# A searched instruction sequence found again under later ends, with ordered start-up work and repeated weight rows loaded as two transfers

## The chip, the cores and the metric

The kernel runs on one core of a Trainium2 chip. A core has five engines that run their own instruction streams: TensorE (PE, matrix products, with a separate row PEld for weight loads), VectorE (DVE), ScalarE (ACT), GpSimd (POOL) and SyncE (SP), which here only issues transfers. Transfers run on 16 DMA engines that all queues of the core share. The metric is device time in microseconds of one execution; the profile is one execution recorded by the hardware.

## What is computed

Two pre-normalised blocks over 2048 rows of 448 features, in bfloat16:

```python
h  = x + A(layernorm(x))        # A: 16 heads of 28; query s looks at keys s, s-2, ..., s-14
h2 = h + B(layernorm(h))
# A:  q,k,v = x@wqkv ; softmax over 8 dilated keys ; o @ wo
# B:  h  = gelu(layernorm(x) @ w1)
#     g0..g3 = the four 112-column quarters of h, shifted by -1, +1, -2, +2 rows
#     x1 = x + concat(g0..g3) @ w2
#     return x1 + gelu(layernorm(x1) @ w3) @ w4        # 448 -> 1792 -> 448
```

## The kernel before

The kernel is written as about 1,090 operations ("ops") that a recording layer collects. Each op has an engine, one or more instructions and the set of ops it depends on. The list `ORDER` near the top of the file is one fixed permutation of all ops, found by an offline search; `schedule` (line 251) walks it, puts each op at the end of its engine's queue, hands out buffers, and estimates start and end times with constants such as `dma_bw` and `lag`. These estimates decide which of the free buffers an op gets and where dummy matmuls ("fillers", `S.filler`) go into gaps of TensorE; the queues themselves follow `ORDER`. `_emit_plan` then derives the semaphore waits. So on each engine the order is frozen, an instruction that waits holds everything behind it on that engine, and nothing is decided at run time. All instructions are recorded through one line, L1039, which is why the profile's groups are told apart by their buffers.

The 2048 rows are 16 tiles of 128, handled in four groups `t` of four tiles. The string `PLAN` names the stages. For attention: `N1 t` (statistics and normalising of x into the buffer `lntm`), `A1 t` (turn `lntm` into `actT`, then queries and keys into `arena`), `V t` (values into `vt`, then copied by transfers into the windowed form `vw`), `A2 t` (on DVE products `qk_r` of 4096 columns, summed per head on PE with the 0/1 matrix `zc`; then softmax and `pb`), `A3 t` (block-diagonal weights `bd_r`, times `vw`) and `O t` (times `wo_s`, plus the residual, into `xin`). For the second block: `B1 t` with `M t` (first MLP with `w1_s`), and then, in units `u` of 3, 4, 4, 4 and 1 tiles, `B2 u`/`T u` (times `w2_s` and the second normalising), `W3 u` (448 to 1792, into `h3T`) and `B3 u` (1792 to 448, into `ost`, then out). In both kernels `phase_W3` forms its products only for units of more than one tile (line 968), so for the last single tile the 448-to-1792 product is left out and `B3` reads what its `h3T` buffers hold.

"Turning" (features onto partitions) is done either on PE (`t` in `TURN`) or by a transposing transfer from SP (`d`): A1 of groups 2 and 3, all of B1, and three of the five B2 units use the transfer. Two strings choose an engine per tile or group: `NORM` for the normalising (`a` ACT, `v` DVE) and `STATS` for the statistics.

The contraction length 448 is three chunks of 128 rows and a rest of 64. `contract` (line 689) runs two products' rests side by side on the two 64-row halves of PE, so the last 64 rows of a weight have to lie on partitions 0 to 63 and again on 64 to 127. `dma_rows` (line 540) loads a weight that way: one transfer `main` for the three chunks, one transfer `rest` for the repeated rows. `rest` reads the same 64 rows twice through an access pattern whose outermost step is `[0, 2]`. The loads are `wqk`, `wv` (from SP), and `w1`, `w3` (from GpSimd), with the rests `wqkr`, `wvr`, `w1r`, `w3r`. For the combined rest of queries and keys, `setup` has GpSimd copy two column blocks of the repeated rows of `wqkv_s` into `wr_s`; a PE group of seven half-height products (64 rows) in A1 waits for these copies.

GpSimd also builds `bmask` (eight dependent `affine_select`s), `zc` (through `indj`, which lives in the buffer `ls`), the mask row of the first window (`maskrow`, ones and -30000s, read by one small matmul of A2 0), and paddings; then it issues the weight loads, the `vw` copies and later the adds of the second residual. In `ORDER` of the kernel before, these set-up instructions are interleaved with the transfers, and `mhalf` and part of `bmask` come as late as after the first `vw` copies.

Of the kernel before, what the change touches and what calls it, by code (L numbers as in the profile page):

```python
# [14 lines left out]
NORM = {'N0': 'aava', 'N1': 'avvv', 'B1': 'avva', 'B2': 'vaava'}  # L15
STATS = {'N1': 'vvva', 'B1': 'vvav', 'B2': 'aavaa'}
# [43 lines left out]
RUNS = {'A3': '1111', 'W3': '24324'}  # L60
# [124 lines left out]
class _Sched:  # L185
# [13 lines left out]
    def group(self, eng, insts, dur, lag=60.0, chan=None, nbytes=0, table=None, after=(), hold=None, pe=()):  # L199
        op = _Op(len(self.ops), self.prio, eng, insts, float(dur), float(lag))  # L200
# [48 lines left out]
    BEHIND = 400.0  # L249

    def schedule(self, dma_bw=190.0, dma_fixed=2000.0, table_load=1300.0):
# [8 lines left out]
        n = len(self.ops)  # L260
# [11 lines left out]
        for idx in ORDER:  # L272
# [13 lines left out]
            if op.is_dma:  # L286
# [3 lines left out]
                if op.nbytes:  # L290
                    dma_free = max(st + op.dur, dma_free) + op.nbytes / dma_bw
                    op.t1 = dma_free + dma_fixed + op.lag
                    if op.eng == "sp":
                        dma_land = max(dma_land, op.t1)
                else:
                    op.t1 = st + op.dur + op.lag
# [102 lines left out]
def bass_sequential_preLN__sliding_local_dilated__mixer_s_mlp__prompt_kernel(  # L399
# [33 lines left out]
    with ExitStack() as es:  # L433
# [106 lines left out]
        def dma_rows(chan, dst, src, lo, n, eng="sp", behind=(), parts=False):  # L540

            last = src[384:448, lo:lo + n]
            def main():
                dma(chan, dst[:, 0:3, :], src[0:384, lo:lo + n].rearrange("(c k) n -> k c n", k=128), 384 * n * 2, eng=eng, behind=behind)
            def rest():
                dma(chan + "r", dst[:, 3, :], bass.AP(last.tensor, last.offset, [[0, 2]] + [list(d) for d in last.ap]),
                    128 * n * 2, eng=eng, behind=behind)
            if parts:
                return main, rest
            main()  # L550
            rest()
# [166 lines left out]
        def setup(after):  # L718
# [3 lines left out]
            for lo in (0, 1):  # L722
                later("tensor_copy", 350, out=wr_s[:, :, 64 * lo:64 * lo + 64], in_=wqkv_s[:, :, 384 + D * lo:448 + D * lo])
# [357 lines left out]
```

## Time and profile before

| what | value |
|---|---|
| median of 3 runs | 209.94 us (207.58, 209.94, 212.35) |
| the profiled execution | 207.0 us; its span from first to last instruction 205.3 us |
| mean granted TensorE clock | 0.983 |
| PE busy | 189.5 us, 1599 matmuls |
| ACT, DVE, POOL busy | 140.2, 123.5, 50.5 us |
| moved by DMA | 17.33 MB in 27079 packets |

In the views that follow, a row of the timeline is: start in us from the first instruction, duration in us, engine, line, operation, output<-inputs, shape, number of merged instructions, and in brackets the idle time of the engine just before it and what ended that. A row of a group is: engine, operation, buffers, shapes, count | busy us in all, mean ns of one | idle us before them. A row of "stretches" is: the window, its length, then the busy time of each engine with the number of its instructions, the granted TensorE clock, the mean busy share of the 16 DMA engines, and GB/s. A row of DMA issues is: output<-input, queue, count, KB of each, median us from issue to landing.

### The profile page before, as it was taken

How to read it: one execution, taken by the hardware profiler on the slowest of the kernel's cores; microseconds unless marked ns; L12 is line 12 of the kernel's file. 1: busy time of each engine (PE TensorE's matmuls, PEld its weight loads, DVE VectorE, ACT ScalarE, POOL GpSimd, SP SyncE). 2: the span in 40 equal slices, each digit the busy share in tenths (PEclk: the TensorE clock that was granted, in tenths of full speed). 3: DMA queues.
4: the chain of work that ended last, by engine and by line, in shares of the span. 5: the costliest groups of instructions: out<-in, count | busy, mean ns of one | idle time of the engine just before them, and what ended most of it. 6: DMA issues, size and time to landing. Idle time of an engine off the chain costs nothing.

```text
span 205.3 us, 3977 instructions
## 1 busy us (share of the span) xinstructions
PE 189.5 (92%) x1599; PEld 90.0 (44%) x1599; DVE 123.5 (60%) x225; ACT 140.2 (68%) x313; POOL 50.5 (25%) x94
## 2 busy tenths in 40 slices
PE   6869699975999499899999999999999999999996
PEld 2445233432434145454455544435544444444563
DVE  7759677998299869999487877570034314310024
ACT  4918699796379669999986975289942497155221
POOL 1239948000630000030083070110050005500040
PEclk9999999997599999999999999999999999999999
DMA  5945359398399500001329060000561002401003
GB/s 156 289 136 154 96 114 221 102 73 84 90 282 362 90 3 0 3 8 27 76 69 151 9 127 24 3 0 0 102 147 48 0 0 51 97 26 45 0 0 112
DMA packets 27079, 17.33 MB, mean 84 GB/s; under 512 B 20443, under 2 KB 25499, under 8 KB 27061
## 3 DMA queue, kind: packets, MB, share of 16 engines
q1 hardware_dynamic: 24388, 9.77, 24.8%
q0 software_dynamic: 2672, 7.32, 12.8%
q8 instruction: 12, 0.20, 0.4%
q14 instruction: 7, 0.05, 0.1%
HBM read 7.91 MB, written 1.84 MB: 47 GB/s over the span
## 4 chain that ended last, share of the span: by engine, by line
PE 69%; ACT 14%; DMA 7%; DVE 5%; issue 4%; POOL 1%; DVEq 0%; POOLq 0%; ACTq 0%
PE ps L1039 69%; DMA actT<-lntm 6%; ACT arena L1039 5%; ACT actT L1039 3%; ACT lntm L1039 2%; DVE qk_r L1039 2%; ACT vt L1039 1%; DMA xin<-in_A_x_dram 1%; DVE lntm L1039 1%; POOL arena L1039 1%; ACT xin L1039 1%; ACT rs_x L1039 1%; DVE st L1039 1%; DVE mx L1039 0%; DVE ls L1039 0%
## 5 line engine op out<-in xcount | busy, mean ns | idle before, releaser
L1039 PE MATMUL ps<-actT,arena 128*128 128x512 bf16 (+4 forms) x348 | 69.0, 364 | 1.6 <-POOL arena L1039 1.6
L1039 PE MATMUL ps<-arena,h3T 128*128 128x448 bf16 (+1 forms) x238 | 46.5, 342 | 0.0
L1039 ACT ACTIVATE h3T<-ps 128x512 bf16<-128x512 f32 (+1 forms) x56 | 28.5, 577 | 24.8 <-PE ps L1039 24.6
L1039 PEld LDWEIGHTS ps<-actT,arena 128*128 128x128 bf16 (+1 forms) x348 | 27.8, 97 | 37.4 <-issue 7.7
L1039 ACT ACTIVATE arena<-ps 128x512 bf16<-128x512 f32 (+4 forms) x64 | 31.3, 524 | 11.6 <-PE ps L1039 10.8
L1039 POOL TENSOR_TENSOR arena<-arena,xin 128x448 f32<-128x448 f32 x16 | 16.4, 1044 | 87.3 <-DVE lntm L1039 49.5
L1039 DVE TENSOR_TENSOR qk_r<-arena 128x4096 bf16<-128x4096 bf16 (+1 forms) x16 | 32.0, 2018 | 1.4 <-PE ps L1039 1.2
L1039 PEld LDWEIGHTS ps<-arena,h3T 128*128 128x128 bf16 x238 | 22.8, 98 | 20.5 <-issue 0.8
L1039 DVE SCALAR_TENSOR_TENSOR ost<-ps,mrs,arena 128x448 bf16<-128x448 f32 (+1 forms) x17 | 11.0, 653 | 29.3 <-POOL mrs L1039 14.0
L1039 ACT ACTIVATE actT<-ps 128x512 bf16<-128x512 f32 (+2 forms) x25 | 15.7, 644 | 14.6 <-PE ps L1039 14.3
L1039 DVE TENSOR_TENSOR bd_r<-arena,bmask 80x2048 bf16<-80x2048 bf16 x16 | 19.6, 1267 | 2.1 <-ACT arena L1039 2.0
L1039 DVE BATCH_NORM_STATS2 st<-xin 128x6 f32<-128x448 bf16 x24 | 14.5, 618 | 6.7 <-ACT xin L1039 4.5
L1039 PE MATMUL ps<-wo_s,actT 128*128 128x448 bf16 x64 | 16.7, 388 | 1.6 <-ACT actT L1039 1.4
L1039 DVE SCALAR_TENSOR_TENSOR arena<-xin,rs_y,ps 128x448 f32<-128x448 bf16 x16 | 10.5, 677 | 12.0 <-PE ps L1039 11.9
L1039 PE MATMUL ps<-actT,w_s 128*112 128x512 bf16 (+1 forms) x64 | 14.7, 388 | 3.1 <-DMA actT<-lntm 3.1
L1039 PE MATMUL ps<-w_s,arena 112*128 112x448 bf16 x64 | 13.8, 353 | 0.3 <-ACT arena L1039 0.3
L1039 POOL DMA_DIRECT2D vw<-vt x15 | 9.0, 603 | 20.7 <-PE ps L1039 18.1
L1039 PE MATMUL ps<-arena,actT 128*128 128x448 bf16 (+1 forms) x64 | 12.6, 354 | 0.5 <-ACT arena L1039 0.5
L1039 POOL TENSOR_TENSOR rs_y<-rs_x,mhalf 128x4 f32<-128x4 f32 (+1 forms) x5 | 4.7, 935 | 28.2 <-DVE rs_x L1039 24.4
L1039 DVE COPY lntm<-lntm 128x256 bf16<-128x256 bf16 (+2 forms) x16 | 4.0, 249 | 11.0 <-ACT lntm L1039 10.7
L1039 PEld LDWEIGHTS ps<-actT,w_s 128*112 128x112 bf16 (+1 forms) x64 | 6.6, 129 | 9.1 <-DMA actT<-lntm 3.5
L1039 ACT ACTIVATE lntm<-arena,nm 128x448 bf16<-128x448 f32 x12 | 7.9, 667 | 3.7 <-DVE nm L1039 3.7
(74 smaller groups left out, 200.1 us busy)
## 6 DMA issues: line engine op xcount, KB each, us to landing
out_dram<-ost SPq DMA_DIRECT2D x15, 112.0 KB, 1.7
arena<-in_B_w_dram POOLq DMA_DIRECT2D x1, 1568.0 KB, 9.3
arena<-in_B_w_dram POOLq DMA_DIRECT2D x1, 1344.0 KB, 11.3
vw<-vt POOLq DMA_DIRECT2D x4, 320.0 KB, 4.5
vw<-vt POOLq DMA_DIRECT2D x4, 256.0 KB, 4.7
xin<-in_A_x_dram SPq DMA_DIRECT2D x2, 448.0 KB, 10.2
xin<-in_A_x_dram SPq DMA_DIRECT2D x3, 224.0 KB, 3.0
arena<-in_A_wqkv_dram SPq DMA_DIRECT2D x1, 672.0 KB, 6.1
```

Of the source, the lines that this page charges most:

```text
L1039: inst = getattr(eng, meth)(**kw)
```

## The change

The search has been run again after the estimates in `schedule` were altered, so `ORDER` is a new permutation, and with it some strings. What else is edited:

```diff
-NORM = {'N0': 'aava', 'N1': 'avvv', 'B1': 'avva', 'B2': 'vaava'}
-STATS = {'N1': 'vvva', 'B1': 'vvav', 'B2': 'aavaa'}
+NORM = {'N0': 'vavv', 'N1': 'avvv', 'B1': 'avva', 'B2': 'vaavv'}
+STATS = {'N1': 'vvva', 'B1': 'vvav', 'B2': 'aaaaa'}
...
-RUNS = {'A3': '1111', 'W3': '24324'}
+RUNS = {'A3': '1111', 'W3': '23334'}
...
-        op = _Op(len(self.ops), self.prio, eng, insts, float(dur), float(lag))
+        op = _Op(len(self.ops), self.prio, eng, insts, float(dur), float(lag + self.LATE * (eng == "pool" and chan is None)))
...
+    SHARED = 1500.0
+    LATE = 300.0
+
+    def schedule(self, dma_bw=240.0, dma_fixed=2000.0, table_load=1300.0):
...
-                    op.t1 = st + op.dur + op.lag
+                    op.t1 = st + op.dur + op.lag + (self.SHARED if dma_free > st else 0.0)
...
             def rest():
-                dma(chan + "r", dst[:, 3, :], bass.AP(last.tensor, last.offset, [[0, 2]] + [list(d) for d in last.ap]),
-                    128 * n * 2, eng=eng, behind=behind)
+                for h in (0, 64):
+                    dma(chan + "r%d" % h, dst[h:h + 64, 3, :], last, 64 * n * 2, eng=eng, behind=behind)
...
-            for lo in (0, 1):
-                later("tensor_copy", 350, out=wr_s[:, :, 64 * lo:64 * lo + 64], in_=wqkv_s[:, :, 384 + D * lo:448 + D * lo])
+            n_ = len(S.ops)
...
                 later("tensor_copy", 168, out=zc[:, :, e, 16 * e:16 * e + 16], in_=indj)
+            for lo in (0, 1):
+                later("tensor_copy", 350, out=wr_s[:, :, 64 * lo:64 * lo + 64], in_=wqkv_s[:, :, 384 + D * lo:448 + D * lo])
...
-
+            early = [op for op in S.ops if op.eng == "pool" and (op.idx < S.phase0 or op.idx >= n_)]
+            for d, op in zip(early, early[1:]):
+                op.odeps.add(d)
+            rest.append(early[-1])
+
+        rest = []
...
-            dma("vwa%d" % sl, vw[PADK:KW, sl, 0:8:2, :], vt[0:64, sl, :, :], 64 * 4096, 600.0, "pool")
+            dma("vwa%d" % sl, vw[PADK:KW, sl, 0:8:2, :], vt[0:64, sl, :, :], 64 * 4096, 600.0, "pool", behind=rest[t:])
...
+        early = [op for op in S.ops if op.eng == "sp"]
+        for d, op in zip(early, early[1:]):
+            op.odeps.add(d)
```

In words: the planner now lets GpSimd's computing end 0.3 us later and a transposing transfer 1.5 us later when ordinary transfers are still under way, and takes 240 instead of 190 GB/s for loads. The repeated rows come by two plain transfers of 64 partitions each. SP's thirteen start-up loads are issued in the order in which they are written, which is the first three x transfers, then `wqk`, then the other x tiles and rests, with the last eight x tiles at the end. GpSimd's set-up runs in the order written: `ident`, `epsilon`, `mhalf`, paddings, all of `bmask`, then (after the normalising of the fourth tile, as before) `indj` and `zc`, the two `wr_s` copies, the mask row, paddings, and only then the loads of `wo`, `w1`, `w2`; the first `vw` copies come behind those.

In the new sequence, as it is built: `w3`'s main load stands on GpSimd right behind the first three `vw` copies, ahead of the copy `vwa0` (before, it was the last load, behind `w4`); the mask-row matmul stands behind V 1 instead of ahead of it; three products of A1 3 stand between the first two groups of A3 0, and so need the second transposing transfer earlier; the five filler matmuls of the kernel before are gone; W3 of unit 1 runs its 14 products in three rounds instead of four, W3 of unit 3 in three instead of two.

More of the change, by code (lines that the diff above doesn't have):

```diff
@@ L249 @@
     BEHIND = 400.0
-    def schedule(self, dma_bw=190.0, dma_fixed=2000.0, table_load=1300.0):
+    SHARED = 1500.0
+    LATE = 300.0
+    def schedule(self, dma_bw=240.0, dma_fixed=2000.0, table_load=1300.0):
         children = [[] for _ in self.ops]
@@ L818, in phase_V @@
                 dma("vwp%d" % sl, vw[0:PADK, sl, 0, :], vt[112:128, 1 - sl, 3, :], PADK * 1024, 600.0, "pool")
-            dma("vwa%d" % sl, vw[PADK:KW, sl, 0:8:2, :], vt[0:64, sl, :, :], 64 * 4096, 600.0, "pool")
-            dma("vwb%d" % sl, vw[0:KW, sl, 1:8:2, :], vt[48:128, sl, :, :], 80 * 4096, 600.0, "pool")
-            last = dma("vwc%d" % sl, vw[0:PADK, sl, 2:8:2, :], vt[112:128, sl, 0:3, :], 16 * 3072, 600.0, "pool")
+            dma("vwa%d" % sl, vw[PADK:KW, sl, 0:8:2, :], vt[0:64, sl, :, :], 64 * 4096, 600.0, "pool", behind=rest[t:])
+            dma("vwb%d" % sl, vw[0:KW, sl, 1:8:2, :], vt[48:128, sl, :, :], 80 * 4096, 600.0, "pool", behind=rest[t:])
+            last = dma("vwc%d" % sl, vw[0:PADK, sl, 2:8:2, :], vt[112:128, sl, 0:3, :], 16 * 3072, 600.0, "pool", behind=rest[t:])
             for which, load in zip(LOADS, (load_w3, load_w4)):
```

76 rows, old and new, of the table ORDER are left out of this document.

## The prediction

> **What bounds the kernel now.** I read the slices of the page first, then the chain of waits in order of time, then stretches of 10 us.
>
> ```profile
> PEclk9999999997599999999999999999999999999999
> PE 69%; ACT 14%; DMA 7%; DVE 5%; issue 4%; POOL 1%; DVEq 0%; POOLq 0%; ACTq 0%
> ...
> 89.73 113.03 PE ps L1039 x751
> ...
> 40.00:50.00 10.00, 6.27 (x128) 3.05 (x126) 9.98 (x8) 8.69 (x21) 0.00 (x0) 0.93 1.11 87
> 50.00:60.00 10.00, 9.88 (x89) 4.00 (x91) 5.21 (x12) 5.12 (x14) 4.76 (x7) 0.73 0.51 139
> 60.00:70.00 10.00, 7.28 (x56) 3.04 (x52) 9.93 (x10) 9.87 (x21) 0.00 (x0) 1.00 1.09 285
> 90.00:100.00 10.00, 10.00 (x76) 4.89 (x75) 9.08 (x10) 9.64 (x28) 0.00 (x0) 1.00 0.28 55
> ```
>
> There are two halves. From 89.73 on, the chain is PE alone for 113.03 us: no wait is left there, and a new order of the same matmuls cannot shorten it. Before that the chain changes hands, and PE loses time in four places: at the start, near 21 us, at 47 to 57 us (the only dip of the granted clock) and at 67 us. What the change is worth is decided there, and a gain there reaches the end whole, because behind it PE runs without a gap.
>
> **The start (A).**
>
> ```profile
> 9.79 2.78 PE L1039 MATMUL ps<-actT,arena 128*128 128x256 bf16 x24
> ...
> 13.33 0.73 POOL L1039 COPY arena<-arena 128x256 bf16<-128x256 bf16 x2 [3.12 <-DMA arena<-in_A_wqkv_dram]
> ...
> 14.12 3.08 PE L1039 MATMUL ps<-actT,arena 64*128 64x512 bf16 x16 [1.55 <-POOL arena L1039]
> ...
> 12.00:14.00 2.00, 0.57 (x6) 0.26 (x3) 1.09 (x4) 0.00 (x0) 0.67 (x2) 1.00 0.24 58
> 42.00:44.00 2.00, 2.00 (x37) 0.74 (x36) 1.98 (x3) 1.88 (x6) 0.00 (x0) 1.00 0.12 50
> ...
> arena<-in_B_w_dram POOLq DMA_DIRECT2D x1, 1344.0 KB, 11.3
> ...
> arena<-in_B_w_dram POOLq DMA_DIRECT2D x1, 448.0 KB, 12.8
> ```
>
> PE has its 24 full products done at 12.57 and stands 1.55 for the half-height ones; GpSimd's two copies stand 3.12 before that, for the repeated rows of `wqk`. While those are awaited the DMA engines are 0.24 busy; while the rest of `w3` is under way (42 to 44), 0.12, which of 16 is two engines. And that rest of `w3` took 12.8 us to land, longer than the 1344 KB of the same weight. So a repeated load, with its outermost step of 2, seems to run on two engines. As two transfers of 64 partitions it should use many. By the 1344 KB row, 448 KB would take some 4 us; I hold 4 to 12.8 as bounds, take the lower, and so let the rows of `wqk` land with the rest of it, about 4 us earlier.
>
> [...]
>
> What is late next is GpSimd itself, since the copies now stand behind `bmask`, `indj` and `zc`:
>
> ```profile
> 8.94 0.51 POOL L1039 MEMSET arena<- 1x512 bf16 x1 [7.27 <-ACT lntm L1039]
> ...
> 14.55 0.19 POOL L1039 TENSOR_SCALAR_AFFINE_SELECT ls<-ls 128x16 bf16<-128x16 bf16 x1
> ...
> L1039 POOL TENSOR_SCALAR_AFFINE_SELECT ls<-ls 128x16 bf16<-128x16 bf16 (+1 forms) x5 | 3.9, 798 | 0.0
> L1039 POOL TENSOR_SCALAR_AFFINE_SELECT bmask<-bmask 80x64 bf16<-80x64 bf16 x8 | 3.5, 432 | 0.5
> ```
>
> GpSimd idled 7.27 until the fourth tile was normalised (8.94); into that the eight `bmask` steps (3.5) fit. Behind it come five `indj` steps: 3.9 as measured, but their mean of 0.80 holds some that ran beside DVE's large products, and 0.19 is what one took alone; so 1.0 to 3.9, plus the fills and copies of `zc`, below 1. Start no later than 8.9, copies 0.73 long: they end between 11.6 and 14.4. DVE has no large product then, so I take the lower end, and the 1.55 goes. The fourth tile's and the first tile's normalising also move from ACT to DVE, which is quicker at it:
>
> ```profile
> L1039 ACT ACTIVATE lntm<-xin,nmr,rs_y 128x448 bf16<-128x448 bf16 x11 | 8.1, 753 | 0.1
> L1039 DVE TENSOR_SCALAR lntm<-xin,mv,rs_y 128x448 bf16<-128x448 bf16 x13 | 4.4, 393 | 3.4 <-ACT rs_y L1039 3.4
> ```
>
> 0.36 less for each of two, 0.7. **A is 2.3** (bounds 0, and 3.0 with twice the 0.7, since three products now also run ahead of the fourth tile's turn).
>
> **The mask row (B).**
>
> ```profile
> 22.67 0.09 POOL L1039 MEMSET arena<- 1x2 bf16 x1
> ...
> 22.91 0.37 PE L1039 MATMUL ps<-arena 1*32 1x512 bf16 x1 [1.94 <-ACT vt L1039]
> ...
> 25.04 0.54 ACT L1039 ACTIVATE vt<-ps 128x448 bf16<-128x448 f32 x1 [1.75 <-PE ps L1039]
> ```
>
> PE stands 1.94 before the mask matmul. The row blames an ACT eviction, but the matmul reads the mask row, whose last memset ended at 22.76; V 1 stands behind it, and ACT then waits 1.75 for V 1. In the new order the mask row is set right behind the copies and its matmul comes after V 1. Late next is ACT, whose evictions the first bracket names. Bounds 0 and 1.94; **I take 1.5**.
>
> **The stall at 47 (C).**
>
> ```profile
> q8 instruction: 1, 0.02, 36.2%
> ...
> 34.31 0.90 POOL L1039 DMA_DIRECT2D arena<-in_B_w_dram  x1
> ...
> 46.39 0.93 PE L1039 MATMUL ps<-wo_s,actT 128*128 128x448 bf16 x4 [0.92 <-ACT actT L1039]
> ...
> 47.44 0.33 PE L1039 MATMUL ps<-bd_r,vw 80*32 80x64 bf16 x20
> 50.12 0.35 PE L1039 MATMUL ps<-bd_r,vw 80*32 80x64 bf16 x12 [2.35 <-issue]
> ...
> 50.40 1.68 PE L1039 MATMUL ps<-wo_s,actT 128*128 128x448 bf16 x4
> 50.52 0.60 ACT L1039 ACTIVATE actT<-ps 128x512 bf16<-128x512 f32 x1 [1.54 <-PE ps L1039]
> ```
>
> PE stops inside a group of 32 whose operands are all there: 20 run, then 2.35 pass with no releaser. The first line is the DMA queue of instructions in the stretch from 47.5 to 47.7: one packet, just as PE runs dry. I read it as a late instruction fetch, held up behind the rest of `w3` (issued at 34.31, landed 12.8 later at 47.1) and the transposing transfer that met it. The clock then falls: the same four products take 1.68 instead of 0.93, and at 0.73 the stretch from 50 to 60 loses 2.7 us of full-speed time. With the split the cause is gone. Not all comes back, because ACT sets the pace there: it lost 1.54 of the 2.35, and half of the 2.7. **C is 1.54 + 1.35 = 2.9** (bounds 0 and 5.05).
>
> [...]
>
> **The wait for B1's turn (D).**
>
> ```profile
> 63.85 6.45 DMA actT<-lntm
> ...
> actT<-lntm SPq DMA_TRANSPOSE x9, 4.6
> ```
>
> This transfer ran beside the loads of `w3` and `w4` (285 GB/s in that stretch) and took 6.45; the median of nine is 4.6. `w3` now comes with the first `vw` copies, and `w4` earlier by as much as A3 0 does. **I take 1.0** of the difference (bounds 0 and 1.85).
>
> **What is added.** The `w3` load moves on GpSimd's queue ahead of `vwa0`, which A3 0 needs:
>
> ```profile
> 28.94 0.70 POOL L1039 DMA_DIRECT2D vw<-vt  x1 [2.59 <-ACT vt L1039]
> ...
> 43.90 0.43 PE L1039 MATMUL ps<-bd_r,vw 80*32 80x64 bf16 x32
> ...
> 53.32 1.82 POOL L1039 DMA_DIRECT2D vw<-vt  x3 [18.11 <-PE ps L1039]
> ...
> vw<-vt POOLq DMA_DIRECT2D x4, 256.0 KB, 4.7
> ...
> DMA to landing us min/median/max: 6.0/6.4/10.6
> ```
>
> The `vw` copies began at 28.94; earlier by A and B, 25.1. Five issues later `vwa0` follows, near 28.5. Behind `w3` it lands at 28.5 + 11.3 + 4.7 = 44.5 at worst; but 11.3 was measured beside `w4`'s load, and half of it gives 38.9. It is needed at 43.90 - 3.8 = 40.1. So 0 to 4.4; **I take 0.7**. The copy that refills the paddings now waits for the first group of A3 0 with `w3`'s second half, `vwb1` and `w4` queued behind it on GpSimd; the queue stood 18.11 before its second round of `vw` copies already, and those loads are wanted late. SP's fixed order costs 0: nothing in it waits, and only group 3's first pass on ACT hangs on its last load. Fillers out, one round of W3 more and one less: 0. The sums of squares of one B2 unit move to ACT, four of 0.67:
>
> ```profile
> L1039 ACT ACTIVATE lntm<-arena,nm 128x448 bf16<-128x448 f32 x12 | 7.9, 667 | 3.7 <-DVE nm L1039 3.7
> ```
>
> They lie beside the gapless PE of the second half and cost 0, or 2.7 if PE should come to wait for ACT there.
>
> **The sum.** 2.3 + 1.5 + 2.9 + 1.0 - 0.7 = 7.0. The profiled execution took 207.0, so 200.0 by it. It lies 2.94 under the median of the runs (209.94); what scatters there I don't know, and I carry half: **201.5**.
>
> **Rivals.**
> 1. The stall of C stays, or falls on another group, since transposing transfers still meet `vw` copies and loads. [...] Against: the packet. 207.0 - (7.0 - 2.9) + 1.5 = 204.4. Chance 0.14.
> 2. `vwa0` is late behind `w3`: 4.4 instead of 0.7, and PE idle that long loses the clock again (2.7): 201.5 + 3.7 + 2.7 = 207.9. For it: the queue's order. Against: the halved 11.3. Chance 0.14.
> 3. Slower: the transposing transfers become the path. Of those between 20 and 80 us the slowest took 10.6, the quickest 6.0.
>
> ```profile
> 33.95 5.78 PE L1039 MATMUL ps<-actT,arena 128*128 128x512 bf16 x28
> ```
>
> PE came to A1 2 at 33.95 without idle time, as its transfer landed, and three products of A1 3 stand between the groups of A3 0, so both transfers are wanted at once, with `w3`'s 1344 KB under way. If both take 10.6, each is 4.6 late and costs the clock: 201.5 + 9.2 + 5.4 = 216.1. It decides as soon as they pass some 6.5. Against: the slow one met the two-engine load; the one beside `w3` and `w4` took 6.45. Chance 0.10.
> 4. The split does nothing, the two engines having another reason: 1.55 and 2.9 go, 201.5 + 4.5 = 206.0. Chance 0.05.
>
> **Chances.** The forecast has 0.57. From all upper bounds (3.0 + 1.94 + 5.05 + 1.85 = 11.8) 195.2 follows, which is the low end; 208.5 takes in rivals 1, 2 and 4. The runs before spread by 2.3% of the median, so 2% is about what can be told from no change: 205.7 and 214.1. Faster: 0.55 of the forecast, 0.10 of rival 1, 0.04 of the others, 0.69. Slower: 0.09, nearly all of rival 3. Within: 0.22.
>
> **What would show it.** PE's half-height products of A1 0 start near 12 with no wait for GpSimd; the rest of `w3`, in halves, lands in some 5 us; no idle PE "issue" time over 1 us, and a clock of 1.0 throughout from 40 to 60; A1 2 begins near 30.2 (33.95 less A and B); PE's gapless stretch begins near 83. I would be wrong if PE waits for `vw` or a transposing transfer in A3 0 (rivals 2, 3), if the copies into `wr_s` end past 14, or if gaps appear behind 90, where I allow none.

## The result, and the profile after

The changed kernel takes 201.03 us (median of 4 runs, 199.47 to 201.89) against 209.03 us (4 runs, 207.58 to 212.35): a ratio of 0.963, with a 95% interval from 0.9525 to 0.9737. The ratio, like all ratios below, leaves out runs over 1.5% above the fastest of the same kernel (here the one of 212.35), so it is not quite that of the medians. The forecast was 201.5. The profiled execution took 199.47, and its span is 197.7 against 205.3.

The slices of the page and the chain that ended last, changed kernel:

```profile
PEclk9999999999999999999999999999999999999999
PE 76%; DMA 9%; DVE 8%; ACT 4%; issue 1%; SPq 0%; ACTq 0%
```

The dip of the clock is gone, and PE carries 76% of the chain instead of 69. Where the time came from is read by cutting both spans at the same three places of the work: the starts of A1 2, M 0 and W3 0 on PE. First the kernel before (columns as in the stretches above: span, busy us of PE, PEld, DVE, ACT and POOL, granted clock, share of the DMA engines, GB/s):

```profile
33.95:70.34 36.39, 29.48 (x301) 12.63 (x301) 31.44 (x38) 28.46 (x63) 6.01 (x11) 0.91 0.84 164
70.34:90.69 20.35, 19.06 (x361) 10.08 (x362) 17.97 (x32) 16.63 (x35) 1.66 (x3) 1.00 0.01 2
90.69:205.20 114.51, 112.89 (x753) 54.63 (x752) 49.94 (x103) 71.56 (x153) 23.34 (x27) 1.00 0.23 50
```

and the same three stretches of the changed one:

```profile
29.41:61.07 31.66, 26.87 (x305) 11.78 (x301) 29.11 (x34) 26.12 (x61) 5.15 (x8) 1.00 0.81 192
61.07:80.30 19.23, 18.10 (x356) 9.64 (x356) 18.38 (x30) 17.71 (x36) 0.00 (x0) 1.00 0.01 3
80.30:197.70 117.40, 113.24 (x763) 55.03 (x755) 50.76 (x104) 73.60 (x161) 25.30 (x29) 1.00 0.22 49
```

Up to A1 2 the change gains 4.54 (33.95 to 29.41). The next stretch gains 4.73 and the third 1.12. The last loses 2.89: 0.35 of it is more work on PE, the rest idle time. Together 7.5. PE's timeline shows where the new idle time lies:

```profile
9.25 5.47 PE L1050 MATMUL ps<-actT,arena 128*128 128x256 bf16 x37
21.32 0.38 PE L1050 MATMUL ps<-arena 1*32 1x512 bf16 x1
39.83 0.43 PE L1050 MATMUL ps<-bd_r,vw 80*32 80x64 bf16 x32
42.82 0.81 PE L1050 MATMUL ps<-actT,arena 128*128 128x512 bf16 x3 [2.56 <-DMA actT<-lntm]
61.07 1.29 PE L1050 MATMUL ps<-actT,w_s 128*112 128x512 bf16 x5 [0.97 <-DMA actT<-lntm]
104.28 0.64 PE L1050 MATMUL ps<-ident,pb 128*80 128x128 bf16 x8 [1.86 <-DVE pb L1050]
```

The products of A1 0, full and half-height, run in one piece from 9.25; the mask matmul has no bracket, so nothing was waited for; no row of 32 is broken by "issue" any more. Two waits over 1 us are new: 2.56 at 42.82 for the second transposing transfer of A1, and 1.86 at 104.28 for a softmax. GpSimd's timeline at the start:

```profile
1.97 3.32 POOL L1050 TENSOR_SCALAR_AFFINE_SELECT bmask<-bmask 80x64 bf16<-80x64 bf16 x8
7.21 1.29 POOL L1050 TENSOR_SCALAR_AFFINE_SELECT ls<-ls 128x64 bf16<-128x64 bf16 x5
9.27 0.74 POOL L1050 COPY arena<-arena 128x256 bf16<-128x256 bf16 x2
```

The copies into `wr_s` end at 10.0 (14.1 before). The DMA issues, with the halves of `wqk` and the main part of `w3`:

```profile
arena<-in_A_wqkv_dram SPq DMA_DIRECT2D x2, 112.0 KB, 5.0
...
arena<-in_B_w_dram POOLq DMA_DIRECT2D x1, 1344.0 KB, 9.7
```

And two steps of the chain in order of time:

```profile
31.28 11.40 DMA actT<-lntm
...
56.54 4.48 DMA actT<-lntm
```

The transfer issued at 31.28 took 11.40 while `w3` and the `vw` copies were under way; that of B1 0, issued at 56.54, took 4.48 (6.45 before).

### The profile page after: what moved, and what is told of

Its sections match the earlier page's. It is cut to its first block, busy times and chain, and to the rows that moved or that the text cites. A ratio compares the mean times of both kernels' runs of the same rounds, so it can differ in the third digit from the quotient of the medians.

```text
span 197.7 us, 3964 instructions
## 1 busy us (share of the span) xinstructions
PE 185.4 (94%) x1594; PEld 89.0 (45%) x1594; DVE 123.2 (62%) x222; ACT 139.8 (71%) x315; POOL 47.5 (24%) x96
## 3 DMA queue, kind: packets, MB, share of 16 engines
q0 software_dynamic: 2080, 7.31, 13.7%
## 4 chain that ended last, share of the span: by engine, by line
PE 76%; DMA 9%; DVE 8%; ACT 4%; issue 1%; SPq 0%; ACTq 0%
PE ps L1050 76%; DMA actT<-lntm 8%; DVE lntm L1050 3%; ACT lntm L1050 2%; DMA xin<-in_A_x_dram 1%; ACT arena L1050 1%; DVE arena L1050 1%; DVE mx L1050 1%; ACT actT L1050 1%; DVE ls L1050 1%; DVE zs L1050 1%; DVE st L1050 1%; SPq L1050 0%; DVE pb L1050 0%; ACT ls L1050 0%
## 5 line engine op out<-in xcount | busy, mean ns | idle before, releaser
L1050 PEld LDWEIGHTS ps<-actT,arena 128*128 128x128 bf16 (+1 forms) x348 | 27.8, 97 | 38.9 <-issue 6.5
L1050 ACT ACTIVATE arena<-ps 128x512 bf16<-128x512 f32 (+5 forms) x64 | 31.5, 520 | 11.6 <-PE ps L1050 11.0
L1050 DVE SCALAR_TENSOR_TENSOR ost<-ps,mrs,arena 128x448 bf16<-128x448 f32 (+1 forms) x17 | 10.8, 653 | 30.9 <-PE ps L1050 28.8
L1050 DVE TENSOR_TENSOR bd_r<-arena,bmask 80x2048 bf16<-80x2048 bf16 x16 | 18.7, 1215 | 3.1 <-ACT arena L1050 3.1
L1050 PE MATMUL ps<-wo_s,actT 128*128 128x448 bf16 x64 | 14.8, 354 | 0.8 <-ACT actT L1050 0.8
L1050 ACT ACTIVATE lntm<-arena,nm 128x448 bf16<-128x448 f32 x16 | 10.5, 660 | 5.3 <-DVE nm L1050 5.3
L1050 DVE COPY lntm<-lntm 128x256 bf16<-128x256 bf16 (+2 forms) x16 | 3.3, 207 | 12.0 <-ACT lntm L1050 11.6
```

The costliest lines, as they stand in the source:

```text
L1050: inst = getattr(eng, meth)(**kw)
```

## Experiments

All of them do the work of the two kernels, which both leave out the 448-to-1792 product of the last tile. Each median stands beside the kernel before in the same comparison, since that kernel alone ranges from 205.5 to 213.7.

**The halves without the order, and the order without the halves.** The loop of the change put into the kernel before, for all four weights and in the old order of everything else:

```diff
-dma(chan + "r", dst[:, 3, :], bass.AP(last.tensor, last.offset, [[0, 2]] + [list(d) for d in last.ap]), ...)
+for h in (0, 64):
+    dma(chan + "r%d" % h, dst[h:h + 64, 3, :], last, 64 * n * 2, eng=eng, behind=behind)
```

> The kernel before, its own order, with every block of repeated rows in two transfers. If the prediction's terms A (its part of the wait, 1.55) and C (2.9) come from the transfers on two engines, PE's wait of 1.55 near 13 us and the stop of 2.35 at 47.8 are gone and the time falls by about 4.5 us. If the stop at 47.8 is due to something else (its place in the program, the transposing transfers), it stays, and only about 1.5 us is gained.

204.03 us (203.10 to 204.99, 4 runs; before 210.83, 7 runs). All four runs lie below the fastest run of the kernel before (205.49). How much of the 6.8 between the medians is the edit's own work and how much the scatter of the clock isn't told by so few runs: the two runs of the kernel before at a granted clock of 0.983 took 205.49 and 207.76, 2.6 more than the mean of these four, and the five at 0.959 to 0.967 took 210.48 to 212.82. The wait near 13 and the stop near 47 are gone, and so is the wait for the mask row. What is late next is B1's turn, for which PE now stands 5.51 instead of 3.06:

```profile
66.12 3.84 PE L1039 MATMUL ps<-actT,w_s 128*112 128x512 bf16 x10 [5.51 <-DMA actT<-lntm]
```

The opposite edit, the lines with "-" in the place of those with "+", in the changed kernel:

> The changed kernel with each block of repeated rows loaded by one transfer again. If the halves carry A and C, the repeated rows of wqk land some 3 us later, PE waits for GpSimd's copies before the half-height products again (1.5 to 2.5 us), and the rest of w3 takes over 10 us to land and starves PE once more near 40 us: 204 to 207 us. If the new order carries the gain and the halves do nothing, the copies end at 10 and the time stays within 0.7 us of the changed kernel's 201.0.

215.33 us (215.11 to 215.61, 4 runs; before 210.83), slower than every run of both kernels and 8 us beyond what I allowed. PE's wait for the copies is back with 0.74 only, for the 1.5 to 2.5 that I expected. The joined rest of `w3` among its DMA issues, PE's wait in the timeline, and two of its stretches:

```profile
arena<-in_B_w_dram POOLq DMA_DIRECT2D x1, 448.0 KB, 18.2
```
```profile
55.82 1.44 PE L1050 MATMUL ps<-actT,arena 128*128 128x512 bf16 x3 [11.90 <-DMA actT<-lntm]
```
```profile
45.00:50.00 5.00, 0.00 (x0) 0.00 (x0) 2.95 (x2) 2.43 (x6) 0.94 (x2) 0.56 1.33 85
50.00:55.00 5.00, 0.00 (x0) 0.00 (x0) 0.00 (x0) 0.00 (x0) 0.00 (x0) 0.50 0.95 99
```

The joined rest of `w3` takes 18.2, and by the chain of waits the transposing transfer that meets it takes 21.64, from 34.05 on. From 50 to 55 every engine stands, the DMA engines move 99 GB/s, and the clock is at half. So the order is worth nothing by itself: alone it costs some 4.5 us by the medians, and the halves are worth 14 us in it, against some 7 in the old order (8.7 and 2.6 if only the kernel before's runs at a clock of 0.983 are counted). The two parts of the change can't be added.

**Which rest does what.** The same loop in the kernel before for `wqk` alone, then for `w3` alone:

```diff
+if chan in ('wqk',):
+    for h in (0, 64):
+        dma(chan + "r%d" % h, dst[h:h + 64, 3, :], last, 64 * n * 2, eng=eng, behind=behind)
+    return
```

> The kernel before with only the repeated rows of wqk in two transfers. If these rows are what the copies wait for, the copies end near 10 instead of 14, PE's wait of 1.55 goes and the first transposing transfer is issued about 1.5 us earlier; the time falls by 1 to 1.6 us unless a later wait takes it back. If GpSimd or the rest of wqk is what ends last, the copies still end near 14 and the time is the same.

206.22 us (204.61 to 207.33, 4 runs; before 210.83). These runs overlap those of the kernel before at a clock of 0.983 (205.49 and 207.76), so the times alone don't tell the two apart; the trace does. The first transposing transfer is issued at 24.73, 3.15 earlier than the 27.88 of before: PE's wait for the copies is gone, and the 1.94 at the mask matmul with it, as the mask row's memsets stand behind the copies on GpSimd. But PE stops longer at the next place:

```profile
44.21 0.33 PE L1043 MATMUL ps<-bd_r,vw 80*32 80x64 bf16 x20
48.21 0.35 PE L1043 MATMUL ps<-bd_r,vw 80*32 80x64 bf16 x12 [3.67 <-issue]
```

The instruction queue from 45.5 to 46.0, and the rest of `w3`, issued at 31.64, in the same view of the DMA queues:

```profile
q8 instruction: 1, 0.02, 12.4%
...
arena<-in_B_w_dram POOLq DMA_DIRECT2D x1, 448.0 KB, 13.5
```

It is the same instruction as before (20 of a group of 32 done, 12 to come), so a place in the program, not a moment. The rest of `w3` lands at 31.64 + 13.5 = 45.1, and only then comes the packet; in the kernel before it landed at 47.1 and the packet came at 47.5.

> The kernel before with only the rest of w3 in two transfers. If that transfer on two engines holds up the instruction fetch, the stop of 2.35 at 47.8 and the low clock behind it go: 2 to 3.5 us faster, the start unchanged. If the two-engine form has nothing to do with the stop, it stays and the time is the same within 1 us.

207.72 us (204.96 to 208.31, 4 runs; before 210.83). The stop is gone, and the packet came at 40.9. Its profiled execution has a span of 205.6 all the same: behind the untouched wait of 1.95 for the mask matmul the clock fell in that run,

```profile
25.00:30.00 5.00, 5.00 (x32) 1.77 (x28) 1.58 (x6) 4.43 (x13) 1.88 (x5) 0.70 0.25 68
```

and B1's turn was waited for 4.45. The medians put the edit at 3, but its runs overlap those of the kernel before at a clock of 0.983, so a gain in time isn't shown; what is shown is that the stop goes with the joined rest of `w3`.

Then the mask row alone, in the kernel before; the memsets are GpSimd's, in their queue:

```diff
-maskrow, ls, maskrow, bmask x2, maskrow, copy, copy, vw, onesrow, ...
+ls, bmask x2, copy, copy, onesrow x2, maskrow x8, vw, ...
```

> The kernel before with the memsets of the mask row put right behind GpSimd's two copies, nothing else. If the mask row is what the mask matmul waits for, PE's idle 1.94 before it goes and the time falls by 1.5 to 2 us, and by some more where the clock would have fallen behind it. If the ACT eviction named in the row holds it up, the 1.94 stays and the time is the same.

207.77 us (205.25 to 211.39, 10 runs; before 209.51, 19 runs; ratio 0.9945, 0.986 to 1.003), which is no difference that can be told. The 1.94 did go, so the mask row it was, and not the ACT eviction that the row names. The first transposing transfer is issued 1.0 earlier. But B1's turn was then waited for 5.03, as with all four halves (5.51) and with those of `w3` (4.45): with `w3` loaded late, a gain ahead of 60 us lets the turn meet more of that load and of `w4`'s, and its transfer took 8.0 to 9.1 in these three, for 6.45. This kernel, with its joined rest of `w3`, also shows no stop; PE's timeline at that instruction, and its DMA queues (the instruction queue from 39 to 40):

```profile
46.76 0.42 PE L1039 MATMUL ps<-bd_r,vw 80*32 80x64 bf16 x32
```
```profile
q8 instruction: 1, 0.02, 6.7%
...
arena<-in_B_w_dram POOLq DMA_DIRECT2D x1, 448.0 KB, 15.2
```

The packet came between 39 and 40 here, ahead of most of the transposing transfer's data, and the rest landed at 47.9. So in these runs the stop came only with the joined rest (0.12 of the 16 DMA engines busy from 42 to 44 in the kernel before), and the joined rest doesn't always bring it.

The packet's time sorts all five kernels. PE goes on 2.6 us after the packet starts in the kernel before (47.5, then 50.1) and 2.4 after it with the halves of `wqk` alone (45.8, then 48.2). In the three without a stop it had started at 36.9, 39.3 and 40.9, over 7 us before PE reached the instruction. In both stops the second transposing transfer of A1 lands just when PE goes on (39.63 + 10.6 and 36.27 + 11.9), but PE doesn't need it there: with the mask row moved, PE passes the place near 47.0, and that transfer lands at 49.6. The view names the queue `instruction`; what the packet holds no view shows, and no row names it as the releaser. So the late fetch stays a reading, the one that fits all five.

**The new wait at 42.8.** First the load of `w3` moved on GpSimd's queue of the changed kernel:

```diff
-vwp1, vwb0, vwc0, w3, vwa1, vwa0, w3r0, refill, vwc1, w3r64, vwb1, ...
+vwp1, vwb0, vwc0, vwa1, vwa0, refill, vwc1, vwb1, w3, w3r0, w3r64, ...
```

> The changed kernel with the three transfers of w3 moved on GpSimd's queue from ahead of vwa0 to behind the refill of the paddings and the vw copies of group 1. If w3's 1344 KB are what makes the second transposing transfer of A1 take 11.40 us, it takes 5 to 7 us, PE's wait of 2.56 at 42.8 goes, and the time is 1 to 2.5 us less, unless w3 then meets the turn of B1 (0.97 of waiting before M 0 becomes 3 or more), which would give it all back. If the vw copies alone make it slow, the 2.56 stays and the time is the same.

205.76 us (201.77 to 207.81, 10 runs; before 209.51). The second transposing transfer of A1 takes 4.3 instead of 11.4 and the wait is gone, but `w3` and `w4` now meet B1's, which takes 8.19 by the chain:

```profile
62.63 3.84 PE L1050 MATMUL ps<-actT,w_s 128*112 128x512 bf16 x10 [4.67 <-DMA actT<-lntm]
```

Both branches of the expectation came true. The order of the change has the cheaper of two collisions.

Then the waiting products moved instead, on PE:

```diff
-A3 0, A1 3 (3 products), A3 0, O 0, ..., A1 3 (3), ...
+A3 0, A3 0, O 0, ..., A1 3 (3 products), A1 3 (3), ...
```

> The changed kernel with the first three products of A1 3, which stand behind the first group of A3 0 on PE, moved behind O 0 next to the other products of A1 3, as they stood in the kernel before. If PE waits there only because they are queued too early, the 2.56 goes and PE has A3 0 and O 0 to do meanwhile: 1 to 2.5 us less. If the work behind hangs on the same transfer, the wait moves to the next products of A1 3 and the time is the same within 0.5 us.

200.33 us (198.48 to 201.84, 4 runs; before 209.51; ratio 0.961, 0.946 to 0.976). Its profiled execution has M 0 at 59.81 for 61.07, so 1.26 of the 2.56; the rest went to the evictions on ACT that PE meets instead. By the times the gain is small: 198.48 and 199.18 at a clock of 1.0, against 199.47 and 199.96 of the changed kernel at that clock. Its chain now runs through `vwa0`:

```profile
27.87 11.01 DMA vw<-vt
```

It lands at 38.9, as the prediction estimated from half of `w3`'s 11.3. PE doesn't wait for it; only ACT's next eviction into `vt` does, for 0.27.

**The wait at 104.** What DVE does ahead of that softmax shows in its timeline in the kernel before and in the changed one, with GpSimd's adds of the second residual beside it in the changed one:

```profile
104.67 1.44 DVE L1039 TENSOR_SCALAR lntm<-xin,nm,rs_y 128x448 bf16<-128x448 bf16 x4
94.83 3.23 DVE L1050 TENSOR_SCALAR lntm<-xin,nm,rs_y 128x448 bf16<-128x448 bf16 x2
95.82 3.12 POOL L1050 TENSOR_TENSOR arena<-arena,xin 128x448 f32<-128x448 f32 x3
```

Before, four normalisings take 1.44 and GpSimd's adds start at 107.77, behind them. In the new sequence the adds fall beside them, and two take 3.23 (1.05 and 2.25). From the maximum of the scores to `pb` DVE needs 10.0 instead of 8.0, about as much more as PE's wait of 1.86.

First, six matmuls of M 2 ahead of the transposes of S 3, in the changed kernel:

```diff
-B3 0 (17), S 3 (8 transposes), M 2 (6), ...
+B3 0 (17), M 2 (6), S 3 (8 transposes), ...
```

> The changed kernel with the first six matmuls of M 2 (0.38 us each, 2.3 together) moved ahead of the eight transposes of S 3 on PE. If PE's wait of 1.86 for the softmax at 104.3 is a matter of order alone, it goes, and with nothing behind it the time falls by 1.5 to 1.9 us. If something behind is late as well, the gain is under 0.5 us.

204.01 us (202.53 to 205.45, 4 runs; before 209.51; ratio 0.986, 0.973 to 0.9996): no gain. M 2 has its own transposing transfer, and that, issued at 104.39, landed no earlier than the softmax was done:

```profile
108.72 1.50 PE L1050 MATMUL ps<-actT,w_s 128*112 128x512 bf16 x6 [2.18 <-DMA actT<-lntm]
```

In that execution B1 0's turn had also cost 2.47 and the clock behind it; that all four runs lie above the changed kernel's isn't explained by the edit alone, and stays open.

**Scatter.** The changed kernel again, in a comparison with the next two:

> The changed kernel itself once more, beside the next two. If its scatter (199.5 to 201.9) is the granted clock alone, each run at a mean clock of 1.0 takes 199 to 200, and each at 0.991 or less 1 to 3 us more.

201.17 us (199.96 to 202.20, 6 runs; before 209.48, 12 runs; ratio 0.967, 0.9613 to 0.9727). One run at a clock of 1.0 took 199.96, five at 0.991 took 201.06 to 202.20. In the profiled one (202.20) the clock falls right behind the wait of 2.51 that ends at 43.0:

```profile
44.00:46.00 2.00, 2.00 (x43) 0.70 (x27) 0.89 (x1) 0.65 (x2) 0.00 (x0) 0.59 0.68 162
46.00:48.00 2.00, 2.00 (x37) 0.87 (x29) 0.63 (x1) 1.08 (x2) 0.00 (x0) 0.56 0.00 0
```

That is 2 x 0.41 + 2 x 0.44 = 1.7 us of full-speed time, about what divides the two groups of runs; a mean of 0.991 is one such stretch in 200 us.

**Towards a better order.** The products of A1 3 moved back as above, and six of B3 0 ahead of S 3:

```diff
-B3 0 (17), S 3 (8 transposes), M 2 (6), ...
+B3 0 (23), S 3 (8 transposes), M 2 (10), ...
```

> The changed kernel with the three products of A1 3 moved back (as before) and six products of B3 0 (0.352 each, 2.1 together) ahead of the transposes of S 3. These hang on w4 and finished work alone, not on a transposing transfer. If the softmax and the transfer for M 2, which lands at 104.8, are the only two things late at 104, both are covered: the wait of 1.86 goes and no new one comes, 1.5 to 1.9 us less than the run with the products of A1 3 alone (196.8 of span at full clock), so a span near 195. If DVE's chain is late for good, a wait comes back behind them.

198.75 us (198.60 to 201.52, 6 runs; before 209.48; ratio 0.958, 0.952 to 0.965). Five of six runs kept a clock of 0.999 to 1.0, with spans of 196.9 to 197.3, so the products of B3 0 brought nothing over the 196.8 of the run with A1 3 alone: the wait for the softmax is 0.72 instead of 1.86, and 0.61 comes back behind it, on ACT.

Then both weights moved away from the transposing transfers. Here the three products of A1 3 stand as in the changed kernel, the six of B3 0 as in the run before, and two other products of B3 0 two groups later:

```diff
-..., w3, vwa1, vwa0, w3r0, refill, vwc1, w3r64, vwb1, vwb0, vwa0, w4, vwc0, vwb1, ...
+..., vwa1, vwa0, refill, vwc1, vwb1, w3, w3r0, w3r64, vwb0, vwa0, vwc0, vwb1, w4, ...
```

> The changed kernel with w3 behind the vw copies of group 1 (issued near 42), w4 held until group 3's first vw copy (near 65), its first two products of B3 0 moved two groups later, and six products of B3 0 ahead of S 3's transposes. If each of the two slow transposing transfers is slow through the weight that is under way beside it, the second of A1 takes some 4.3 us and that of B1 0 some 4.5 us, both waits of PE (2.56 and 0.97) go, and the span is 193.5 to 196. If the vw copies or the transfers themselves are enough to make B1's transfer slow, it stays over 7 us and PE waits 3 or more before M 0: a span of 199 or more. If w4 comes too late, PE waits for it in B3 0.

199.39 us (198.95 to 204.21, 6 runs; before 209.48; ratio 0.960, 0.954 to 0.9655). M 0 starts at 59.07, the two transfers took 4.5 and 4.2; but `w4`, issued at 80.15, met the turn of B1 1, which was issued at 83.08 and took 8.18:

```profile
91.30 1.07 PE L1050 MATMUL ps<-actT,w_s 128*112 128x512 bf16 x4 [2.34 <-DMA actT<-lntm]
...
93.83 3.02 POOL L1050 TENSOR_TENSOR arena<-arena,xin 128x448 f32<-128x448 f32 x3
96.60 0.70 DVE L1050 TENSOR_SCALAR lntm<-xin,nm,rs_y 128x448 bf16<-128x448 bf16 x2
```

The last two rows are a test of the wait at 104 that nobody planned: with PE late by this wait, GpSimd's adds were nearly over when DVE came to its normalisings. Two took 0.70, the way to `pb` 8.2, and PE didn't wait for S 3, where the run before waits 0.72 with the same products ahead.

Last, `w4` into the gap between the two turns:

```diff
-..., vwb0, vwa0, vwc0, vwb1, w4, ...
+..., vwb0, vwa0, vwc0, vwp1, w4, ..., vwb1, ...
```

> The run before with w4 released one step earlier, behind vwp1, which waits for the first group of A3 1 (62.4 in that run) instead of group 3's vw copy (79.5). It should then load from 63 to 73, between the turn of B1 0 (done at 59) and that of B1 1 (issued at 83). If a transposing transfer is slow only while a weight loads beside it, B1 1's takes 4 to 5 us instead of 8.18, PE's wait of 2.34 at 91.3 goes, and the span at full clock falls from 197.4 to 194.5 to 196. If B1 1's transfer is slow for another reason, the wait and the 197.4 stay.

198.40 us (198.10 to 199.06, 6 runs; before 207.59, 11 runs; ratio 0.9554, 0.9518 to 0.9591), better than the changed kernel. `w4` is issued at 64.04, and the transposing transfers ahead of 100 us take 4.3 to 5.6; of the waits for them 0.76 is left, before M 0:

```profile
59.87 2.07 PE L1050 MATMUL ps<-actT,w_s 128*112 128x512 bf16 x10 [0.76 <-DMA actT<-lntm]
103.66 0.64 PE L1050 MATMUL ps<-ident,pb 128*80 128x128 bf16 x8 [1.12 <-DVE pb L1050]
```

All six runs had a clock of 1.0. The spans are 196.4 to 197.3, not the 194.5 to 196 that I gave: S 3 still waits 1.12 for DVE, whose way to `pb` takes 10.8 here, with two normalisings of 4.03 together beside GpSimd's adds.

## Why the prediction was right, step by step

The total came within 0.5 us, but not by its terms as they stood: two of them were too small and one cost was missed, and these nearly cancel. That it is so close is in part luck. Two of the prediction's own signs of being wrong came: PE waits for a transposing transfer inside A3 0, and there is a gap behind 90.

- **A and B** (2.3 + 1.5 = 3.8): 4.54 in the trace. The mechanisms hold. The halves of `wqk` alone bring 3.15 of it, since the mask row only waited in GpSimd's queue behind the copies; so B needed no move of its own. The remaining 1.4 lies in the rest of the start (loads, normalising on DVE); it wasn't tried by itself.
- **C** (2.9): 2.35 of stop and, by PE's busy time in the stretch to M 0, 29.48 - 26.87 = 2.61 of slower clock, 4.96 in all. The step that failed is the discount "because ACT sets the pace there": ACT lost its time to the same cause and got it back. That a late instruction fetch stood behind it isn't shown, but fits all five kernels of the old order: the stop, of 2.35 and 3.67 us, is at one place of the program, came only with the joined rest, and ends 2.4 to 2.6 behind the packet.
- **D** (1.0): 3.06 - 0.97 = 2.09. It was sized as an excess over a median. The runs show more: in the old order gains ahead went in part into this wait (5.51, 5.03, 4.45), and in the new order it comes back when `w3` is moved late again (4.67). So moving `w3` early is what lets A, B and C be kept.
- **What is added** (0.7 for `vwa0`): 2.56, and by another way. `vwa0` landed when it was estimated (38.9, in the run with A1 3 moved); the second transposing transfer of A1 was late, at 11.40. This is rival 3 at one of its two places, with 2.56 instead of 4.6 and, in the profiled execution, no loss of clock. With a joined rest the same place costs 11.90 and more clock (215.33).
- **Behind 90 us, "where I allow none"**: wrong. The stretch from W3 0 gave back 2.89, of which 1.86 is the softmax of S 3. In the trace of the kernel before, S 3's transposes start at 111.81 behind 18 products of B3 0 and without idle time; the new order has 17 there, and PE is at them 1.86 ahead of DVE. What the prediction put at nothing is that in the new order GpSimd's adds meet DVE's normalisings ahead of that softmax: two took 3.23, and in the run in which they took 0.70 PE had no wait there.
- **Rivals 2 and 4**: `vwa0` was not late, and the halves did land sooner: those of `wqk` in 5.0; those of `w3` in 6.0 to 7.3 in the old order, for the 4 that I took, against 12.8 to 15.2 joined. In the changed kernel itself they took 11.1, behind `w3`'s main part, and 3.3, so the sign "in some 5 us" held for the one issued last only. How many engines a half uses alone isn't shown; while the last half and window copies were under way in the changed kernel, from 43 to 45, 0.71 to 0.98 of the 16 were busy.
- **The sum**: 3.8 + 2.9 + 1.0 - 0.7 = 7.0 foreseen. Measured: 4.54, then 4.96 + 2.09 - 2.56 with 0.24 of smaller waits, 1.12 up to W3 0 (0.96 of it work that PE does elsewhere), less 2.89: 7.5.
- **The 1.5 on top** had no cause given. The runs give one: of the ten of the changed kernel, the two at full clock took 199.5 and 200.0, the eight at 0.991 took 200.6 to 202.2, and where such a run was profiled the clock fell behind the wait at 42.8.

## What to carry to other kernels

Read a transfer's price in company: put the issue and landing of each latency-critical transfer beside the loads under way at that time, and place big loads into the gaps between them, first of all where a faster part upstream will move one onto the other. A load whose outermost dimension is 2 is cheap to write, took 12.8 to 18.2 us here for 448 KB, and held up others far beyond its size: the second transposing transfer of A1 took 10.6 beside it in the kernel before, and 4.9 with all the halves, which land sooner. That it held up an instruction packet too is a reading of two stops. Look at what GpSimd does beside a DVE instruction before taking over its time into another order. A wait of PE of 2.51 us cost 1.7 more in clock here, and one of 2.56 at the same place none, so judge an edit by several runs and their clocks and not by one profile.

## What was not expected of the hardware

A transposing transfer of one group (128 x 448 in four tiles, 448 KB) took 4.3 to 4.4 us with neither a weight nor the window copies under way (the changed kernel from 105 us on), and 4.6 to 6.7 beside the window copies (the first of A1 in the five kernels of the old order). It took 6.3 to 9.1 beside `w3` and `w4` or `w4` alone, and 4.3 to 6.0 where only the last 2 us of `w4` were left. It took 10.6 to 11.9 beside the joined rest of `w3` or beside its 1344 KB with the `vw` copies, and 21.6 beside all of these. The plain window copies of 256 KB slowed as well, from 4.8 in the kernel before to 10.7 beside `w3`'s 1344 KB in the changed one. So what the traces show is the price in company: 8.2 beside a weight for the transfer that takes 4.3 alone.

A normalising on DVE (128 x 448, bfloat16) ahead of the softmax of S 3 took 0.38 to 0.48 us in the kernel before. In the changed kernel, one ran beside GpSimd's adds of 128 x 448 in float32 for over 2 us, and it took 2.25; in the run with `w4` in the gap two took 4.03 together. Why isn't shown.

The granted clock fell behind an idle time of PE of 2.51 us in one profiled execution of the changed kernel and not behind 2.56 in the other. By the clock records of the traces it is half while it is low, and the low stretches last 3.41 us or a whole multiple of it: 3.41 in the second profile of the changed kernel, 6.83 from 48.67 on in the kernel before, 13.7 in the changed one with the joined rest (a clock of 0.56, 0.50 and 0.57 in the three stretches of 5 us from 45 on). The falls lie a whole multiple of 3.41 behind the start of the first clock record, in the kernel before thirteen times, from 4.30 to 48.67, and in the second profile of the changed kernel eleven times, from 6.80 to 44.35:

```profile
40.94:44.35 3.41, 1.36 (x37) 0.70 (x38) 3.41 (x3) 2.37 (x7) 2.14 (x4) 1.00 0.48 123
44.35:47.76 3.41, 3.41 (x41) 1.36 (x40) 1.16 (x2) 1.62 (x3) 0.00 (x0) 0.50 0.28 65
```

So the same wait can lie between two such instants or be cut by one. In the 3.41 us ahead of this fall PE was busy for 1.36. In the first profile, counted in the same steps from its first record at 4.33, the wait was cut at 41.88, the stretches on either side had 1.79 and 2.47 of work, and the clock stayed. That the work between two instants decides is a reading, and what share of it would isn't shown: in the kernel before, the fall came behind a stretch with 1.59 of work, and one with 1.54, from 65.74 on, had none behind it.
